# Interleaved H3 and S4D layers: one-pass gated update, angles rounded on ScalarE, and intermediate arrays stored in the order of their reading

## The chip, the cores and the metric

The kernel runs on one core of one Trainium2 chip. The core has a matrix engine (TensorE; PE in the profile, PEld for its weight loads), three engines for elementwise work (VectorE, DVE; ScalarE, ACT; GpSimd, POOL), and a SyncE queue (SP) that issues nearly all transfers; sixteen DMA engines carry them. The metric is device microseconds of one execution, lower is better. Everything is float32.

## The reference

A sequence of 2048 positions and 512 channels goes through four layers, A, B, A, B, each with a layer norm in front and a residual around it.

```python
def _A_ref(q, k, v, shift_k, ssm_k, ssm_D):      # q is layernorm(x)
    kv = short_causal_conv(k, shift_k) * v
    y = irfft(rfft(kv padded) * rfft(ssm_k padded))[:S]
    return q * (y + kv * ssm_D)
def _B_ref(u, ...):                              # u is layernorm(x)
    dt = exp(log_dt); A = -exp(log_A_real) + 1j * A_imag; C = (C_real + 1j * C_imag) * dt
    K = 2 * real(sum_n C[d, n] * exp(A[d, n] * dt * l))
    return irfft(rfft(u padded) * rfft(K padded))[:L] + u * D_skip
x = A_q
x = x + _A_ref(layernorm(x), ...); x = x + _B_ref(layernorm(x), ...)
x = x + _A_ref(layernorm(x), ...); x = x + _B_ref(layernorm(x), ...)
```

The convolution of layer A doesn't depend on x, so its result y is computed once and used twice; each use is a "gated update", x + layernorm(x) * y.

## The kernel before

Both long convolutions are Fourier transforms of length 4096 done as matrix products, in four quarters of 128 channels. A quarter's spectrum has 8 chunks; a chunk is 128 partitions (the real parts of 64 frequencies, then their imaginary parts) by 4 x 128 values, 256 KB.

The program is built of steps that a scheduler lays out ahead of the run; each engine then works its list in order.

- **Taps** (taps, 64 steps). For layer B the tap values K come from 128 modes per channel. `angles` makes phases with a matmul into PSUM (`pa`), rounds them to whole turns by adding and taking off a large constant (`MAGIC`) on DVE (tile `y`, L482), and takes the whole turns off with a second matmul by minus the identity (L483). `waves` takes Abs and two Sin on ACT; `mags` takes Exp; `products` multiplies on DVE and POOL; `contract` sums the modes on PE (`pk`), and DVE scales by 2 dt into `ks` (L528, L529), which goes to DRAM.
- **Spectra** (spectrum_quarter). Chunk by chunk ACT copies the transform `pu` into `pc` (two buffers, L244), and SP stores it into the DRAM array `spec` (L245). `spec[0]` is layer A's, from the inputs, at the start; `spec[1]` layer B's, a quarter after each 16 steps of the taps.
- **Convolutions** (convolution). 32 steps each, one chunk a step: `kab` is loaded from `spec` into both halves of the partitions, real and imaginary parts side by side, by two transfers of 256 KB, one for each half of the partitions (L259); DVE multiplies `pu` by it (`vv`, L278), ACT makes the swapped product's operand (`sw`), POOL multiplies and adds; PE transforms back. Convolution A (beside the taps) stores its result to `ya_d` in DRAM (L656); convolution B runs twice, three loads ahead, with four buffers of `kab`.
- **Gated updates** (gated_update, twice, 16 rows of 128 x 512). `yaq` is loaded from `ya_d` (L703). In one of three ways, by a table of letters, a row is shifted by minus its mean (`nm`) and multiplied by y into `ut`: on DVE in one pass (L714), or ACT and POOL (L717, L720), or POOL twice (L719, L720). DVE then adds ut times the inverse deviation (`rs`) to x, with the row's sum (L721), and ACT squares for the variance (L723). A `normalizer` per 8 rows makes nm, rs and nb.

The four transfers rows_d<-hl (L359), at the start, carry the modes' parameters to DRAM. SP issues its transfers in order; one that waits holds up those behind it. So does an engine's instruction that waits for a transfer.

Of the kernel before, what the change touches and what calls it, by code (L numbers as in the profile page):

```python
# [9 lines left out]
F32 = mybir.dt.float32  # L10
F32R = mybir.dt.float32r
# [9 lines left out]
NQ = 4  # L21
# [78 lines left out]
def kernel(ctx: ExitStack, tc: tile.TileContext, out, x_in, kv_in, ssmk_in, ssmd_in,  # L100
# [24 lines left out]
    TP = (0, 1)  # L125
    WAYS1 = "cbcdcbcdcbcdcbcd"
    WAYS2 = "bcdbcbcbbcbbcbcb"
    NORM1 = "SVSVSVSVSVSVSVSV"
# [71 lines left out]

    def normalizer(t0, n, st=None):
# [16 lines left out]
    def spectrum_quarter(which, q, src, pool, zlast, zb, tag):  # L220
        z = pool.tile([128, 64, 32, 2], F32, name="zk", tag="z", bufs=zb)
        dr = pool.tile([1, 128], F32, name="dr", tag="dr", bufs=1)
        nc.sync.dma_start(dr, (ssmd_in, dsk_in)[which][:, 128 * q:128 * q + 128])
        for g in range(4):
            kk = pool.tile([128, 512], F32, name="kk", tag="kk", bufs=3 - which)
            nc.sync.dma_start(kk, src[4 * q + g])
# [12 lines left out]
        for c in range(NCH):  # L239
            pu, ins = f2_chunk(z, c, None, tag)  # L240
            if c == NCH - 1:
                zlast.append(ins)
            pc = pool.tile([128, CK * 128], F32, name="pc", tag="pc", bufs=2)
            S.copy(pc, pu.rearrange("p k c -> p (k c)"))  # L244
            nc.sync.dma_start(spec[which][q][c], pc)  # L245
            yield
# [3 lines left out]
    def convolution(which, pools, steps, finish, lag, ahead, nk, ns, nw, inplace, add_dve, zlast=None, late_step=None, first_b=False):  # L250
# [3 lines left out]
        def load(s):  # L254
            q, c = divmod(s, NCH)
            pool = pools["conv"]
            kab = pool.tile([128, 2, CK, 128], F32, name="kab", tag="kab", bufs=nk)
            for h in range(2):
                (G if first_b and s < GL else nc.sync).dma_start(kab[64 * h:64 * h + 64].rearrange("p r k c -> p r (k c)"),  # L259
                                  spec[which][q][c].rearrange("(r k) x -> k r x", r=2))  # L260
# [73 lines left out]
    G.memset(warm, 0.0)  # L334
    S.activation(warm, warm, AF.Exp)
    dt = gp.tile([128, 4], F32, name="dt")
    nc.sync.dma_start(dt, ldt_in)
    nc.sync.dma_start(flat(cr), cr_in)
# [7 lines left out]
    dt2 = gp.tile([128, NQ, 32], F32, name="dt2")  # L346
    halfpi = gp.tile([128, 1], F32, name="halfpi")
    G.memset(halfpi, math.pi / 2)

    minus = gp.tile([128, 128], F32R, name="minus")  # L350
    G.dma_start(minus, minus_in)

# [14 lines left out]
    across = lambda t_: t_[:, :, None].to_broadcast([128, 4, 128])  # L367
    S.activation(dt, dt, AF.Exp)
    S.activation(la, la, AF.Exp)
# [33 lines left out]
    V.scalar_tensor_tensor(t1, t3, 0.5, t1, op0=ALU.mult, op1=ALU.add)  # L403
    V.tensor_add(t2, t2, t1)

# [11 lines left out]
    nc.sync.dma_start(flat(dt2), ldtb_in[:, None, :].to_broadcast([4, 32, 128]))  # L417
    S.activation(dt2, dt2, AF.Exp)
    V.tensor_scalar_mul(dt2, dt2, 2.0)
    nctx.close()  # L420
# [22 lines left out]
    rows, ms, xys, pks, angs = {}, {}, {}, {}, {}  # L443
    NXY = 2
    NM1 = 9
    NM2 = 5
# [27 lines left out]
    def angles(gi, k):  # L474
        h, s = divmod(k, 2)
        hs = slice(64 * h, 64 * h + 64)
        pa = pp.tile([128, 512], F32, name="pa", tag="pa", bufs=NPA)
        T.matmul(pa, rows[gi][hs, 0, :], tabs["tt"][hs, 8 * s:8 * s + 8, :], start=True, stop=False,
                 skip_group_check=True)

        y = wk.tile([128, 512], F32R, name="y", tag="y", bufs=2)
        V.tensor_scalar(y, pa, MAGIC, MAGIC, op0=ALU.add, op1=ALU.subtract)  # L482
        T.matmul(pa, minus, y, start=False, stop=True, skip_group_check=True)  # L483
        angs[gi, k] = pa

    def waves(gi, k):
# [4 lines left out]
        S.activation(co, rv, AF.Abs)  # L491
        for i in (S.activation(tt[:, 1, :, 1:65], rv, AF.Sin, scale=TWO_PI),  # L492
                  S.activation(co, co, AF.Sin, scale=-TWO_PI, bias=halfpi)):  # L493
            after(i, last_exp[0])
            last_sin[0] = i
# [15 lines left out]
    def contract(gi, k):  # L511
# [10 lines left out]
        if k < 3:  # L522
            return
        q, g = divmod(gi, 4)
        ks = wk.tile([128, 64, 8], F32, name="ks", tag="ks", bufs=2)
        d2 = dt2[:, q, 8 * g:8 * g + 8][:, :, None].to_broadcast([128, 8, 32])
# [62 lines left out]
    with ExitStack() as actx:  # L589
# [107 lines left out]
    def gated_update(buffer, spare, rnd, load_x=False):  # L697
        yas = []
        for k in range(4):
            if load_x:  # L700
                nc.sync.dma_start(x[:, 4 * k:4 * k + 4, :], x_in[:, 4 * k:4 * k + 4, :])
            ya = buffer(k)
            nc.sync.dma_start(ya.rearrange("p g t c -> p g (t c)"),  # L703
                              ya_d[:, :, 128 * k:128 * k + 128].rearrange("g p x -> p g x"))
            yas.append(ya)
        ways, cold = (WAYS1, WAYS2)[rnd], (WU1, WU2)[rnd]
        for t in range(16):
            pool, tag, bufs = spare[t % len(spare)]
            ut = pool.tile([128, 512], F32, name="ut", tag=tag, bufs=bufs)

            groups = lambda a: a.rearrange("p (g c) -> p g c", c=32)
            y = yas[t // 4][:, :, t % 4, :]
            if ways[t] == "c":
                V.scalar_tensor_tensor(groups(ut), groups(x[:, t, :]), nm[:, t:t + 1], y, op0=ALU.add, op1=ALU.mult)  # L714
            else:
                if ways[t] == "b":
                    S.activation(ut, x[:, t, :], AF.Identity, bias=nm[:, t:t + 1])  # L717
                else:
                    G.tensor_scalar(ut, x[:, t, :], nm[:, t:t + 1], None, op0=ALU.add)  # L719
                G.tensor_mul(groups(ut), groups(ut), y)  # L720
            V.scalar_tensor_tensor(x[:, t, :], ut, rs[:, t:t + 1], x[:, t, :], op0=ALU.mult, op1=ALU.add,  # L721
                                   accum_out=mv[:, t, 0:1])
            S.activation(ut, x[:, t, :], AF.Square, scale=-512.0, bias=mv[:, t, 0:1], accum_out=mv[:, t, 1:2])  # L723

# [15 lines left out]
    own = [(xp, "ut", 3)] * 3  # L740
    def normalized(rows):
        for t in rows:
            if t % UN == UN - 1:
                last_root[0] = normalizer(t + 1 - UN, UN)

    with ExitStack() as yctx:
        yp = sbuf(yctx, "yp", "right")
        normalized(gated_update(lambda k: yp.tile([128, 16, 4, 32], F32, name="yaq", tag="yaq", bufs=NYA),
                                own + [(yp, "ut", 16 - 4 * NYA)] * (16 - 4 * NYA), 0, True))
    bq = sbuf(ctx, "conv_q", "right")  # L750
    pools = {}
    turn = {"u": 0, "zu": 0}


# [7 lines left out]
    def steps_b(rnd, q):  # L762
# [3 lines left out]
        def norm(c):  # L766
            for t in (2 * c, 2 * c + 1):
                eng = "S" if q > 1 else NORMQ[rnd][t] if q else (NORM1, NORM2)[rnd][t]
                if eng != "S":
# [76 lines left out]
    normalized(gated_update(lambda k: rotating("u", [128, 16, 4, 32], "yaq", 3),  # L846
                            own + [(pools["conv"], "vv", NSB)] * NSB + [(pools["conv"], "sw", NSB)] * NSB, 1))
    for _ in conv_b(1):
# [66 lines left out]
```

## Time and profile before

| | |
|---|---|
| median of 3 runs | 800.36 us (798.78 to 801.9) |
| the profiled execution | 805.59 us, of which its span is 803.8 us |
| moved by DMA | 135.47 MB, mean 169 GB/s |
| mean granted TensorE clock | 0.877 |

The profile is of one execution. A row of a table by stretches has the stretch in us, its length, each engine's busy time with its count of instructions, the granted TensorE clock, the busy share of the 16 DMA engines, and GB/s. A group of instructions has its line, engine, operation, out<-in, shapes and count, then the busy time in all and the mean ns of one, then the engine's idle time just before them. A row of the SP queue has the start, the time and the transfer.

### The profile page before, as it was taken

To read this page: it belongs to the slowest core of one execution; us is meant where nothing else is said; L and a number is where in the kernel's file an instruction comes from. 1 tells how busy PE (TensorE), PEld (TensorE's weight loads), DVE (VectorE), ACT (ScalarE), POOL (GpSimd) and SP (SyncE) were. 2 spreads that over 40 slices of the span, in tenths; PEclk is the share of its full clock that TensorE was granted. 3 is DMA by queue.
4 is the path that set the end of the run, shared out by engine and by line. 5 is a ranking of instruction groups with operands and counts; after the bars stand their busy time and mean duration, and the time that the engine had idled before them with its cause. 6 is when DMAs were issued, how large, how long until landed. Compare 5 with 4: busy or idle time off the path is not lost. (4 is left out here: it accounts for less than half of the span.)

```text
span 803.8 us, 14448 instructions
## 1 busy us (share of the span) xinstructions
PE 635.2 (79%) x5064; PEld 447.3 (56%) x5064; DVE 621.3 (77%) x939; ACT 477.7 (59%) x879; POOL 533.7 (66%) x496
## 2 busy tenths in 40 slices
PE   3378696688799989999889863599789750998996
PEld 2255565356567747767556442386657620476673
DVE  7757979998967967647759499845668889878776
ACT  4035355345378875776785765649746525878573
POOL 4965778776778965838956277316665836288783
PEclk9676599868999999999899665789989995899999
DMA  9577177367477463664441593147987642068792
GB/s 326 188 247 270 40 241 254 108 200 254 146 215 203 127 182 110 182 171 123 115 131 34 174 341 105 46 129 199 233 200 183 159 103 54 1 164 223 201 252 105
DMA packets 89612, 135.47 MB, mean 169 GB/s; under 512 B 8508, under 2 KB 37700, under 8 KB 89028
## 3 DMA queue, kind: packets, MB, share of 16 engines
q1 hardware_dynamic: 88644, 132.13, 56.5%
q0 software_dynamic: 896, 2.43, 1.1%
q8 instruction: 40, 0.66, 0.4%
q14 instruction: 32, 0.26, 0.1%
HBM read 98.87 MB, written 35.65 MB: 167 GB/s over the span
## 5 line engine op out<-in xcount | busy, mean ns | idle before, releaser
L280 POOL TENSOR_TENSOR sw<-sw,kab 128x512 f32<-128x512 f32 x96 | 124.4, 1302 | 67.6 <-ACT sw L277 59.6
L196 PEld LDWEIGHTS pu<-zu,w 128*128 128x128 f32 x768 | 95.7, 193 | 52.9 <-DVE vv L278 18.6
L196 PE MATMUL pu<-zu,w 128*128 128x128 f32 x768 | 109.5, 285 | 15.1 <-DVE vv L278 12.8
L504 POOL TENSOR_TENSOR xy<-tt,m 128x512 f32<-128x512 f32 x64 | 84.9, 1327 | 53.5 <-ACT tt L493 23.8
L171 PE MATMUL pf<-kk,wz 128*128 128x256 f32 x256 | 86.3, 481 | 41.8 <-POOL kk L236 25.3
L278 DVE TENSOR_TENSOR vv<-pu,kab 128x512 f32<-128x512 f32 x96 | 64.9, 679 | 63.9 <-ACT sw L277 27.0
L290 PE MATMUL pi<-vv,mm 128*128 128x128 f32 x768 | 107.3, 285 | 3.5 <-DVE vv L278 2.6
L281 POOL TENSOR_TENSOR vv<-vv,sw 128x512 f32<-128x512 f32 x76 | 98.8, 1303 | 13.6 <-DVE vv L278 10.3
L290 PEld LDWEIGHTS pi<-vv,mm 128*128 128x128 f32 x768 | 96.5, 197 | 15.0 <-issue 9.1
L276 ACT ACTIVATE sw<-pu 64x512 f32<-64x512 f32 x96 | 57.0, 594 | 63.3 <-PE pu L196 60.8
L171 PEld LDWEIGHTS pf<-kk,wz 128*128 128x128 f32 x256 | 56.7, 237 | 62.3 <-POOL kk L236 33.3
L491 ACT ACTIVATE tt<-pa 128x512 f32<-128x512 f32 x64 | 38.3, 599 | 82.1 <-PE pa L483 72.3
L196 PE MATMUL pu<-zk,w 128*128 128x128 f32 x512 | 78.3, 307 | 6.4 <-DVE zk L191 4.2
L196 PEld LDWEIGHTS pu<-zk,w 128*128 128x128 f32 x512 | 72.7, 217 | 15.6 <-DVE zk L191 6.3
L505 DVE TENSOR_TENSOR tt<-tt,m 128x512 f32<-128x512 f32 x64 | 79.9, 1248 | 0.9 <-ACT tt L493 0.4
L244 ACT COPY pc<-pu 128x512 f32<-128x512 f32 x64 | 37.4, 591 | 57.3 <-PE pu L196 35.3
L506 DVE SCALAR_TENSOR_TENSOR xy<-tt,m 128x256 f32<-128x256 f32 x64 | 51.5, 805 | 25.7 <-ACT tt L492 15.3
L468 ACT ACTIVATE m<-pm 128x512 f32<-128x512 f32 x96 | 53.8, 604 | 22.6 <-PE pm L466 21.6
L483 PE MATMUL pa<-y,minus 128*128 128x512 f32 x64 | 37.1, 588 | 32.0 <-DVE y L482 30.5
L311 PE MATMUL po<-w,w 128*64 128x512 f32 x192 | 55.4, 655 | 7.3 <-DVE w L305 7.0
L519 PE MATMUL pk<-xy,tt 128*32 128x64 f32 x2048 | 50.5, 242 | 13.3 <-DVE ks L529 9.0
L519 PEld LDWEIGHTS pk<-xy,tt 128*32 128x32 f32 x2048 | 37.7, 122 | 39.1 <-issue 28.9
(139 smaller groups left out, 1295.4 us busy)
## 6 DMA issues: line engine op xcount, KB each, us to landing
kab<-spec SPq DMA_DIRECT2D x188, 256.0 KB, 4.0
spec<-pc SPq DMA_DIRECT2D x64, 256.0 KB, 2.7
kvt<-kv_in SPq DMA_DIRECT2D x16, 624.0 KB
yaq<-ya_d SPq DMA_DIRECT2D x8, 1024.0 KB, 10.6
kk<-ssmk_in SPq DMA_DIRECT2D x16, 256.0 KB, 2.9
kv_d<-u SPq DMA_DIRECT2D x16, 256.0 KB, 7.5
kdram<-ks SPq DMA_DIRECT2D x64, 64.0 KB, 1.8
kk<-kdram SPq DMA_DIRECT2D x16, 256.0 KB, 2.7
```

Of the source, the lines that this page charges most:

```text
L171: yield T.matmul(o, w, rhs, start=True, stop=True)
L196: ins = T.matmul(pu[:, i, :], w2[:, c * CK + i, :], z[:, :, c * CK + i, :], start=True, stop=True)
L276: S.mul(sw[0:64], pu[64:128], -1.0)
L278: V.tensor_mul(vv, pu, kabs[s][:, 0])
L280: (V if last else G).tensor_mul(sw, sw, kabs[s][:, 1])
L281: (V if last or s % add_dve == add_dve - 1 else G).tensor_add(vv, vv, sw)
L290: i1s[t] = T.matmul(pi[:, i, :], mm[:, c * CK + i, :], vvs[t][:, i, :], start=True, stop=True)
L311: ins = T.matmul(po[64 * a:64 * a + 64], w4, ws[g][:, :, 16 * a:16 * a + 16, :].rearrange("p x t r -> p t x r"), start=True, stop=True, ti ...
L468: i = S.activation(m, pm, AF.Exp)
L504: G.tensor_mul(xy[:, :, :, 32:64], tt[:, :, :, 1:33], m1[:, :, 32:64][:, None].to_broadcast([128, 2, 8, 32]))
L505: (G if (4 * gi + k) % E2P == E2P - 1 else V).tensor_mul(e2, e2, m2[:, None].to_broadcast([128, 2, 8, 32]))
L519: T.matmul(pk[32 * i4:32 * i4 + 32, 2 * k + i, :], e2[:, r, 4 * i + i4, :], xy[:, r, 4 * i + i4, :], start=r == 0, stop=r == 1, tile_posit ...
```

## The change

It has six parts.

1. **Gated update in one pass.** ACT makes `ut` = 1 + rs * y; DVE makes x = (x + nm) * ut with the row's sum. The result lacks the row's mean, which the next layer norm doesn't see; `off` keeps the sum of both means, and ACT adds it to whole rows in the last convolution (its third quarter). In the second update the last 8 rows get their statistics from DVE instead of ACT's square.
2. **Angles.** ACT adds MAGIC (activation Identity with a bias), DVE forms (y - MAGIC) - pa in one pass, and the second matmul goes; Abs and Sin read SBUF, not PSUM.
3. **2 dt inside log|C|.** log 2 + log dt is added to the logarithm of C's magnitude at the start; the copies of `pk` are plain ones, one on DVE and one on ACT.
4. **Spectrum as it is read.** `spec` keeps real and imaginary parts of a frequency side by side in DRAM: [chunk, 64, 2, 512]. The store swaps the two outer dimensions, and one transfer with a source broadcast to both halves of the partitions loads `kab`.
5. **y as it is read.** `ya_d` is [4, 128, 16, 128]: it is written in pieces of 512 B, and each of yaq's loads reads 8 KB in a row.
6. The last spectrum quarter's `pc` takes the nine buffers of a tile of the taps that is done with.

```diff
-    spec = [[dram.tile([NCH, 128, CK * 128], F32, name=f"spec{i}_{q}") for q in range(NQ)] for i in range(2)]
+    spec = [[dram.tile([NCH, 64, 2, CK * 128], F32, name=f"spec{i}_{q}") for q in range(NQ)] for i in range(2)]
-    ya_d = dram.tile([16, 128, 512], F32, name="ya_d")
+    ya_d = dram.tile([4, 128, 16, 128], F32, name="ya_d")
...
+            if which == 1 and q == NQ - 1:
+                pc = wk.tile([128, CK * 128], F32, name="pc", tag="m1", bufs=NM1)
+            else:
+                pc = pool.tile([128, CK * 128], F32, name="pc", tag="pc", bufs=2)
             S.copy(pc, pu.rearrange("p k c -> p (k c)"))
-            nc.sync.dma_start(spec[which][q][c], pc)
+            nc.sync.dma_start(spec[which][q][c].rearrange("k r x -> r k x"), pc)
...
-            for h in range(2):
-                (G if first_b and s < GL else nc.sync).dma_start(kab[64 * h:64 * h + 64].rearrange("p r k c -> p r (k c)"),
-                                  spec[which][q][c].rearrange("(r k) x -> k r x", r=2))
+            (G if first_b and s < GL else nc.sync).dma_start(
+                kab.rearrange("p r k c -> p (r k c)"),
+                spec[which][q][c].rearrange("k r x -> k (r x)")[None].to_broadcast([2, 64, 2 * CK * 128]))
...
-    V.tensor_add(t2, t2, t1)
+    V.tensor_scalar(ldt, ldt, math.log(2.0), None, op0=ALU.add)
+    for g in range(4):
+        V.scalar_tensor_tensor(t2[:, g], t2[:, g], ldt[:, g:g + 1], t1[:, g], op0=ALU.add, op1=ALU.add)
...
-        y = wk.tile([128, 512], F32R, name="y", tag="y", bufs=2)
-        V.tensor_scalar(y, pa, MAGIC, MAGIC, op0=ALU.add, op1=ALU.subtract)
-        T.matmul(pa, minus, y, start=False, stop=True, skip_group_check=True)
+        y = wk.tile([128, 512], F32, name="y", tag="y", bufs=NY)
+        S.activation(y, pa, AF.Identity, bias=magic)
+        V.scalar_tensor_tensor(y, y, MAGIC, pa, op0=ALU.subtract, op1=ALU.subtract)
...
-        V.tensor_mul(kv_[:, :, 32:64], pk[:, :, 0:32], d2)
-        V.tensor_mul(kv_[:, :, 31::-1], pk[:, :, 32:64], d2)
+        V.tensor_copy(kv_[:, :, 32:64], pk[:, :, 0:32])
+        S.copy(kv_[:, :, 31::-1], pk[:, :, 32:64])
...
-            nc.sync.dma_start(ya_d[4 * q + g], ya)
+            nc.sync.dma_start(ya_d[:, :, 4 * q + g].rearrange("k p x -> p k x"), ya.rearrange("p (k x) -> p k x", k=4))
...
+            S.activation(groups(uts[t]), yas[t // 4][:, :, t % 4, :], AF.Identity, scale=rs[:, t:t + 1], bias=1.0)
...
+            V.scalar_tensor_tensor(x[:, t, :], x[:, t, :], nm[:, t:t + 1], ut, op0=ALU.add, op1=ALU.mult,
+                                   accum_out=mv[:, t, 0:1] if t < BN[rnd] else None)
+            if t < BN[rnd]:
+                S.activation(ut, x[:, t, :], AF.Square, scale=-512.0, bias=mv[:, t, 0:1], accum_out=mv[:, t, 1:2])
             else:
+                V.bn_stats(st0[:, t, :], x[:, t, :])
...
+                    if q == 2:
+                        S.activation(x[:, t, :], x[:, t, :], AF.Identity, bias=off[:, t:t + 1])
```

What stands where on the queues follows; a row is a line, an operation, what it writes and reads, and the shape written (outermost dimension first), with the count of equal ones in a row.

First SP, near the start, which the change leaves alone: the loads of the inputs and tables (kk, w, kvt), and the first three of the stores rows_d<-hl. Before:

```order
L226 DMA kk<-ssmk_in 128x512
L359 DMA rows_d_99<-hl 8x16x1024
L667 DMA w_104<-w_in 128x1024 x2
L602 DMA kvt<-kv_in 128x1248
L223 DMA dr<-dsk_in 1x128
L226 DMA kk<-ssmk_in 128x512 x2
L359 DMA rows_d_98<-hl 8x16x1024 x2
```

The store rows_d has 8 in its outermost dimension on the DRAM side; the loads around it have 128.

Then SP from the last quarter of layer B's spectrum through the first convolution B to the first loads of the second one (spec_0 to spec_3 are the quarters; the rows of kab up to the last are the first convolution B). Before:

```order
L245 DMA spec_3_64<-pc 128x512 x8
L259 DMA kab<-spec_0_61 64x2x512 x12
L259 DMA kab<-spec_1_62 64x2x512 x6
L703 DMA yaq<-ya_d 128x16x128
L259 DMA kab<-spec_1_62 64x2x512 x2
L703 DMA yaq<-ya_d 128x16x128
L259 DMA kab<-spec_1_62 64x2x512 x8
L259 DMA kab<-spec_2_63 64x2x512 x14
L703 DMA yaq<-ya_d 128x16x128
L259 DMA kab<-spec_2_63 64x2x512 x2
L259 DMA kab<-spec_3_64 64x2x512 x16
L259 DMA kab<-spec_0_61 64x2x512 x8
```

With the change:

```order
L252 DMA spec_3_64<-pc 2x64x512 x8
L265 DMA kab<-spec_0_61 128x1x1024 x6
L265 DMA kab<-spec_1_62 128x1x1024 x3
L707 DMA yaq<-ya_d 128x2048
L265 DMA kab<-spec_1_62 128x1x1024 x2
L707 DMA yaq<-ya_d 128x2048
L265 DMA kab<-spec_1_62 128x1x1024 x3
L265 DMA kab<-spec_2_63 128x1x1024 x7
L707 DMA yaq<-ya_d 128x2048
L265 DMA kab<-spec_2_63 128x1x1024
L265 DMA kab<-spec_3_64 128x1x1024 x8
L265 DMA kab<-spec_0_61 128x1x1024 x4
```

The order is the same; each pair of loads is one transfer, and the store writes 2 x 64 x 512 where it wrote 128 x 512. The first two loads of convolution B (four transfers before) stand on POOL's queue. The source of a load, which these rows don't show, is 64 x 2 x 512 before and 2 x 64 x 1024 now, with step zero in the dimension of 2.

Last, DVE in the first gated update, among the last taps (tt, xy, y, ks) and the spectrum's transposes (zk). Before:

```order
L482 TENSOR_SCALAR y<-pa 128x512 x2
L714 SCALAR_TENSOR_TENSOR ut<-x,nm,yaq 128x512 x2
L505 TENSOR_TENSOR tt_225<-tt_225,m_4394 128x16x32
L721 SCALAR_TENSOR_TENSOR x,mv<-ut,rs,x 128x512 x2
L528 TENSOR_TENSOR ks<-pk,dt_135 128x8x32
L529 TENSOR_TENSOR ks<-pk,dt_135 128x8x32
L506 SCALAR_TENSOR_TENSOR xy<-tt_225,m_4402 128x8x32
L721 SCALAR_TENSOR_TENSOR x,mv<-ut,rs,x 128x512 x2
```

With the change:

```order
L489 SCALAR_TENSOR_TENSOR y<-y,pa 128x512
L729 SCALAR_TENSOR_TENSOR x,mv<-x,nm,ut 128x512 x3
L512 SCALAR_TENSOR_TENSOR xy<-tt_230,m_4380 128x8x32
L511 TENSOR_TENSOR tt_230<-tt_230,m_4376 128x16x32
L729 SCALAR_TENSOR_TENSOR x,mv<-x,nm,ut 128x512 x2
L512 SCALAR_TENSOR_TENSOR xy<-tt_224,m_4384 128x8x32
L729 SCALAR_TENSOR_TENSOR x,mv<-x,nm,ut 128x512 x2
```

The passes that wrote ut are gone from DVE; x takes one pass a row.

More of the change, by code (lines that the diff above doesn't have):

```diff
@@ L125 @@
     TP = (0, 1)
[L126 to L127 removed]
+    GA = 3
+    BN = (16,8)
     NORM1 = "SVSVSVSVSVSVSVSV"
@@ L199, in f2_chunk @@
         return pu, ins
+    off = cpool.tile([128, 16], F32, name="off")
     def normalizer(t0, n, st=None):
@@ L444 @@
     NXY = 2
+    NY = 2
     NM1 = 9
@@ L702, in gated_update @@
             ya = buffer(k)
[L703 to L704 removed]
+            nc.sync.dma_start(ya.rearrange("p g t c -> p (g t c)"), ya_d[k].rearrange("p g x -> p (g x)"))
             yas.append(ya)
[L706 to L723 removed]
@@ new lines, in gated_update, with factor @@
+        cold = (WU1, WU2)[rnd]
+        groups = lambda a: a.rearrange("p (g c) -> p g c", c=32)
+        uts = {}
+        def factor(t):
+            pool, tag, bufs = spare[t % len(spare)]
+            uts[t] = pool.tile([128, 512], F32, name="ut", tag=tag, bufs=bufs)
+            S.activation(groups(uts[t]), yas[t // 4][:, :, t % 4, :], AF.Identity, scale=rs[:, t:t + 1], bias=1.0)
+        if rnd == 0:
+            G.tensor_scalar(off, nm, -1.0, None, op0=ALU.mult)
+        else:
+            for t0 in range(0, 16, HN):
+                G.tensor_sub(off[:, t0:t0 + HN], off[:, t0:t0 + HN], nm[:, t0:t0 + HN])
@@ L740, with normalized @@
     own = [(xp, "ut", 3)] * 3
-    def normalized(rows):
+    def normalized(rows, rnd):
         for t in rows:
             if t % UN == UN - 1:
-                last_root[0] = normalizer(t + 1 - UN, UN)
+                last_root[0] = normalizer(t + 1 - UN, UN, None if t < BN[rnd] else lambda i: st0[:, i, :])
     with ExitStack() as yctx:
@@ L767, in norm @@
             for t in (2 * c, 2 * c + 1):
+                nb = nbs[0]
+                if rnd == 1 and q > 1:
+                    nb = nbs[1]
+                    if q == 2:
+                        S.activation(x[:, t, :], x[:, t, :], AF.Identity, bias=off[:, t:t + 1])
                 eng = "S" if q > 1 else NORMQ[rnd][t] if q else (NORM1, NORM2)[rnd][t]
@@ L846 @@
     normalized(gated_update(lambda k: rotating("u", [128, 16, 4, 32], "yaq", 3),
-                            own + [(pools["conv"], "vv", NSB)] * NSB + [(pools["conv"], "sw", NSB)] * NSB, 1))
+                            own + [(pools["conv"], "vv", NSB)] * NSB + [(pools["conv"], "sw", NSB)] * NSB, 1), 1)
+    nbs.append(cpool.tile([128, 16], F32, name="nb2"))
+    G.tensor_mul(nbs[1], off, rs)
+    G.tensor_sub(nbs[1], nb, nbs[1])
     for _ in conv_b(1):
```

31 lines of the change are left out of this document (15 added, 16 removed).

## The prediction

> **What bounds the kernel now.** I read the page's head, then the chain of work that ended last, then busy time by stretches.
>
> ```profile
> span 803.8 us, 14448 instructions
> PE 635.2 (79%) x5064; PEld 447.3 (56%) x5064; DVE 621.3 (77%) x939; ACT 477.7 (59%) x879; POOL 533.7 (66%) x496
> DVE 14%; PE 14%; issue 7%; ACT 5%; POOL 5%; DMA 3%; SPq 0%; DVEq 0%; POOLq 0%; ACTq 0%
> ```
>
> PE and DVE share the chain and the DMA has 3% of it: today this is a kernel of engines. (The chain covers the second half; records are missing before.) The next table cuts the span where the spectra's transfers begin and end: 0 to 47 setup; to 210 the spectrum of layer A is stored; to 413 convolution A loads it, and half of layer B's spectrum is stored; to 544 the tail of the taps, the first gated update and the other half; to 641 the loads of the first convolution B; to 706 its end and the second gated update; then the second convolution B. The last three columns are the granted clock, the share of the 16 DMA engines, and GB/s.
>
> ```profile
> 0.00:47.00 47.00, 18.92 (x72) 14.20 (x72) 32.24 (x44) 12.53 (x19) 30.21 (x40) 0.85 0.73 248
> 47.00:210.00 163.00, 129.47 (x1036) 89.34 (x1036) 146.34 (x186) 77.19 (x134) 120.27 (x107) 0.79 0.60 196
> 210.00:413.00 203.00, 186.36 (x1829) 135.09 (x1828) 145.47 (x205) 146.23 (x254) 145.56 (x137) 0.97 0.57 163
> 413.00:544.00 131.00, 94.32 (x853) 66.28 (x852) 99.33 (x149) 78.99 (x156) 68.09 (x63) 0.77 0.43 131
> 544.00:641.00 97.00, 83.39 (x542) 62.03 (x540) 67.94 (x116) 64.08 (x120) 66.71 (x59) 0.95 0.81 201
> 641.00:706.00 65.00, 34.82 (x156) 17.73 (x152) 58.65 (x151) 37.84 (x90) 30.40 (x31) 0.79 0.20 50
> 706.00:804.00 98.00, 87.92 (x587) 62.59 (x585) 71.30 (x93) 60.81 (x110) 72.45 (x64) 0.99 0.71 194
> ```
>
> DVE fills 47 to 210, PE the three convolutions, DVE the gated updates. But the DMA engines are never far off: 0.57 to 0.81 of them are busy while spectra move. So the first question on this change is how many DMA engines its new transfers use, and only then what it saves on DVE and PE.
>
> **What one transfer gets of the DMA engines.** Almost every transfer of the kernel before has 32, 64 or 128 entries in its outermost dimension, on both sides. One large one hasn't: the store rows_d<-hl (L359), 512 KB, goes out as 8 x 16 x 1024, outermost 8. It is issued at 12.95 and at 21.95; after that SP issues nothing until 31.4 (the second of the pair). The queue's rows and the stretches behind them:
>
> ```profile
> 12.95 0.65 SPq L359 DMA_DIRECT2D rows_d<-hl  x1
> 18.15 2.77 SPq L226 DMA_DIRECT2D kk<-ssmk_in  x2
> 21.95 10.01 SPq L359 DMA_DIRECT2D rows_d<-hl  x2
> ...
> 20.00:22.00 2.00, 0.52 (x3) 0.12 (x1) 2.00 (x2) 0.37 (x1) 2.00 (x3) 1.00 1.03 421
> 22.00:23.00 1.00, 0.00 (x0) 0.00 (x0) 1.00 (x2) 0.00 (x0) 1.00 (x1) 0.93 0.97 380
> 23.00:24.00 1.00, 0.00 (x0) 0.00 (x0) 1.00 (x2) 0.00 (x0) 1.00 (x2) 0.50 0.62 250
> 24.00:25.00 1.00, 0.00 (x0) 0.00 (x0) 1.00 (x2) 0.20 (x1) 1.00 (x1) 0.50 0.49 196
> 25.00:26.00 1.00, 0.03 (x1) 0.03 (x1) 1.00 (x2) 0.00 (x0) 1.00 (x3) 0.50 0.52 205
> 26.00:27.00 1.00, 1.00 (x3) 0.82 (x4) 1.00 (x2) 0.00 (x0) 1.00 (x1) 0.50 0.53 214
> 27.00:28.00 1.00, 1.00 (x4) 0.82 (x3) 1.00 (x2) 0.00 (x0) 1.00 (x2) 0.50 0.47 190
> 28.00:29.00 1.00, 1.00 (x4) 0.82 (x3) 1.00 (x1) 0.00 (x0) 0.83 (x1) 0.50 0.28 115
> ```
>
> Until 23 the queue drains on all engines (1.03, 0.97), at 421 / (16 x 1.03) = 25.5 KB per us and engine. From 24 to 28 exactly half are left (0.49, 0.52, 0.53, 0.47), at 190 / (16 x 0.47) = 25.3 each. The rows from 24 to 29 carry 196 + 205 + 214 + 190 + 115 = 920 KB, about the two stores' 1,049 KB. I read it so: a transfer is dealt over as many engines as its outermost dimension has entries, always the same first ones; two stores of outermost 8 put 131 KB extra on each of eight engines, 5.2 us at 25.3. That is what the half share lasts.
>
> The change makes two frequent transfers with an outermost dimension of 2: the spectrum's store (2 x 64 x 512 on the DRAM side) and the load of kab (a source broadcast to 2 x 64 x 1024). By this reading both run on the same **two** engines of sixteen.
>
> The Trainium skill, "DMA: Bandwidth & Descriptors", section "Why a DMA increments its semaphore by 16 and not by 1", states the same as a rule: the largest number up to 16 that divides the slowest dimension of both sides, on the lowest-numbered engines. The half share agrees for 8; no run shows 2. That page's table of specifications gives some 27 GiB/s (29 KB per us) for an engine; by it a load of kab would take 9.0 us and the sum below come to about 1,430; the rows give 25.3, and I go by them.
>
> **The change part by part.** First the sizes.
>
> ```profile
> q1 hardware_dynamic: 88644, 132.13, 56.5%
> kab<-spec SPq DMA_DIRECT2D x188, 256.0 KB, 4.0
> spec<-pc SPq DMA_DIRECT2D x64, 256.0 KB, 2.7
> 531.88 12.41 SPq L245 DMA_DIRECT2D spec<-pc  x8
> L259 SPq DMA_DIRECT2D kab<-spec x188: 573/580/4378, 210.0 to 779.5; - x188
> ```
>
> *Load of kab.* 512 KB per step in one transfer instead of two of 256 KB that land 4.0 us after issue. On two engines: 262.1 KB each / 25.3 = **10.4 us**, for a step that now takes (641 - 544) / 30 = 3.2 us. 96 loads: 995 us. *Store of a spectrum chunk.* 131.1 KB on each of two engines: **5.2 us**; 64 stores: 332 us. Both bounds of the rate: above, 214 / 8 = 26.7 if just eight engines carried the best half-share row (9.8 us a load); below, the last stretch of the table, mostly kab loads, 194 / (16 x 0.71) = 17.1 (15.3 us a load, 7.7 a store). I take 25.3, since two engines can't crowd each other as sixteen do there.
>
> All other SP transfers still use sixteen engines, but each puts a sixteenth on the crowded two and lands only when that is through. By stretch, with what stays in force:
>
> - 0 to 47: no spectrum moves, 47.
> - 47 to 210: the pair gets 32 stores, 166, and its part of the rest, (163 x 196 KB - 32 x 262) / 16 / 25.3 = 58: 224 at least. At most 163 + 166 = 329, if nothing lay beside the stores. In each quarter's eight stores ACT stands at the copy into the two buffers of pc, and PE behind it, while DVE's and POOL's gating of kv goes on; so nearer the lower end: **240**.
> - 210 to 413: 32 loads 332 + 16 stores 83 + rest (203 x 163 - 16,777 - 4,194) / 16 / 25.3 = 30, together 444; the engines' 203 lies beneath. DVE's product with kab waits in order, and behind it the taps' products, so a few gaps: **460**.
> - 413 to 544: pair 83 + 30, less than the engines' 131. The first gated update gives 7 back (below); the last eight stores take 42 where they took 12.4 to issue, and the last landing 2, so 28 more, and the loads of kab stand behind them on SP: 131 - 7 + 28 = **152**.
> - 544 to 641: 30 loads 311 + three yaq loads 8 = **319**.
> - 641 to 706: the second update gives 5 back; the four loads issued there (42) fit beneath: **60**.
> - 706 on: 28 loads 290 + output stores 5 = **295**, then the 20 us that now follow the last load's landing (803.8 - 779.5 - 4.0).
>
> Sum 47 + 240 + 460 + 152 + 319 + 60 + 295 + 20 = 1,593. The profiled execution was 805.59 us, 1.8 over its span, and 5.2 over the median of the runs, 800.36: **1,590**.
>
> *The rest of the change*, from the groups of instructions (the first three rows in the first gated update, the fourth in the second) and the waits:
>
> ```profile
> 467.00:512.00 45.00, 19.48 (x260) 12.94 (x259) 45.00 (x59) 23.89 (x50) 36.34 (x28) 0.65 0.56 173
> L714 DVE SCALAR_TENSOR_TENSOR ut<-x,nm,yaq 128x512 f32<-128x512 f32 x8 | 14.9, 1899 | 0.0
> L720 POOL TENSOR_TENSOR ut<-ut,yaq 128x512 f32<-128x512 f32 x8 | 11.9, 1498 | 1.0 <-ACT ut L717 1.0
> L714 DVE SCALAR_TENSOR_TENSOR ut<-x,nm,yaq 128x512 f32<-128x512 f32 x6 | 7.5, 1295 | 0.0
> L723 ACT ACTIVATE ut<-x,mv 128x512 f32<-128x512 f32 x32 | 22.9, 715 | 28.2 <-DVE x L721 28.1
> L626 DVE BATCH_NORM_STATS2 st<-xt 128x6 f32<-128x512 f32 x16 | 10.6, 665 | 0.0
> L483 PE MATMUL pa<-y,minus 128*128 128x512 f32 x64 | 37.1, 588 | 32.0 <-DVE y L482 30.5
> L491 ACT ACTIVATE tt<-pa 128x512 f32<-128x512 f32 x64 | 38.3, 599 | 82.1 <-PE pa L483 72.3
>   ACT pc L244: 20.5, 7
>   DMA kab<-spec: 42.0, 22
> ```
>
> First update: DVE, full for 45 us, loses 8 passes, 14.9; ACT gains 13 factors of about 0.7, 9, and the new rounding: 24 becomes some 38. So 45 falls to 38: 7 (bounds 0 and 15). Second: DVE loses 7.5 and POOL's contention, gains 8 statistics x 0.67 = 5.3: 5 (0 to 8). The angles: PE loses 37 us, ACT gains 64 x 0.6 = 38 and dearer reads, DVE swaps one pass for one. The stores of ya in 512 B pieces, the copies of ks, log 2 dt, nine buffers for the last pc (of ACT's 20.5 us of waits for spec stores) and ACT's 16 additions of the offset (11 us): I count all at nothing, because the engines wait for the pair anyway; without that cover they are worth what the first rival says.
>
> **Rivals.** *The transfers spread over sixteen engines after all* (faster): half a share was another queue's tail, or the pair changes from transfer to transfer. Against it, 920 KB came out at half share with nothing else issued. Then -7, -5, the angles -5 (between -20 and +10: PE is full for much of 210 to 413, ACT's added latency eats it), fewer waits for spec stores -3 and for kab -5 of 42, offset +2: 800 - 23 = 777. It decides if the dealing is by the total number of pieces (128) and not by the outermost count. *Only the store narrows* (slower): the zero-step dimension of the broadcast doesn't count and kab is dealt by 64. Then 47 + 240, 203 + 2 bursts x 19 = 241, 152, and the last 260 less 5 and 5 for kab: 930. The trace has no broadcast large enough to tell. *The pair is also slow* (17.1 KB per us): 47 + 331 + 671 + 171 + 472 + 60 + 436 + 20 = 2,208; it is the upper end of the main case.
>
> **How the numbers follow.** Two engines for both 0.85, store alone 0.06, no narrowing 0.08, anything else 0.01. The forecast is the likeliest, 1,590. Its low end: every burst hidden (224, 444, 131, 55) gives 1,535, and at 26.7 the four transfer-bound stretches lose 67: 1,470. Its high end 2,200. That holds about 0.94 of the main case, 0.80 in all. A measurement of this kernel can tell about 0.5%, 4 us: faster 0.08, within it 0.01, slower 0.91.
>
> **What would show it.** Right: kab lands more than 10 us after issue in the convolutions; in the first convolution B the DMA share is near 2/16 = 0.13 and some 50 GB/s, where 0.81 and 201 stood; the chain is mostly "DMA kab<-spec"; every engine is under half busy; setup unchanged. Wrong: a share over 0.5 in the convolutions, or kab landing in 4 us (first rival); stores late but kab prompt (second). If loads take 15 us, the rate was wrong, not the mechanism.

## The result and the profile after

| | before | after |
|---|---|---|
| median of the runs made side by side | 801.13 us (4 runs, 798.78 to 805.56) | 1604.98 us (4 runs, 1602.92 to 1607.36) |
| ratio, 95% interval | | 1.998 (1.989 to 2.006) |
| the profiled execution (its span) | 805.59 us (803.8) | 1603.58 us (1601.7) |

The forecast was 1,590. Some executions of any of these kernels come out 1 to 2% longer, among them the profiled one with both transfers wide (813.12 us); medians and ratios below leave these out, while the 808 of the expectations is a median with them. The page of the changed kernel, in the parts that were read of before: span, busy time, the DMA queue, and the chain that ended last, by engine and by line.

```profile
span 1601.7 us, 14220 instructions
PE 789.0 (49%) x5000; PEld 554.7 (35%) x5000; DVE 575.4 (36%) x920; ACT 543.4 (34%) x977; POOL 487.1 (30%) x476
q1 hardware_dynamic: 63548, 132.05, 23.4%
DMA 67%; PE 10%; ACT 6%; DVE 5%; issue 5%; SPq 4%; POOL 3%; DVEq 0%; POOLq 0%; ACTq 0%
DMA kab<-spec 38%; DMA spec<-pc 14%; DMA out_dram<-yo 3%; DMA kk<-kdram 3%; PE pf L171 3%; PE pu L196 2%; DMA yaq<-ya_d 2%; DMA xt<-x_in 2%; DMA u<-kv_d 1%; PE po L318 1%; DMA kdram<-ks 1%; SPq L660 1%; PE pm L473 1%; PE pk L525 1%; DMA kk<-ssmk_in 1%
```

The same 132 MB move, in fewer packets, and yet the chain went from 3% DMA to 67%, and no engine is busy for half the span. Here are the stretches, cut at the same events as the prediction's steps (columns as there):

```profile
0.00:53.00 53.00, 20.08 (x71) 15.14 (x72) 39.51 (x51) 14.37 (x22) 34.19 (x45) 0.81 0.69 237
53.00:280.00 227.00, 139.57 (x1022) 96.85 (x1021) 136.88 (x183) 93.45 (x161) 110.50 (x100) 0.69 0.41 133
280.00:748.00 468.00, 239.70 (x1929) 172.62 (x1929) 147.56 (x214) 180.38 (x307) 154.01 (x151) 0.69 0.21 73
748.00:888.00 140.00, 79.26 (x735) 54.43 (x733) 62.19 (x116) 94.35 (x188) 36.51 (x39) 0.72 0.34 117
888.00:1211.00 323.00, 130.83 (x544) 96.15 (x544) 72.48 (x119) 56.40 (x101) 66.81 (x60) 0.62 0.16 61
1211.00:1298.00 87.00, 35.67 (x128) 19.00 (x129) 46.38 (x148) 43.38 (x91) 13.12 (x21) 0.70 0.11 37
1298.00:1584.00 286.00, 133.97 (x538) 94.44 (x536) 62.57 (x84) 58.20 (x105) 66.87 (x60) 0.63 0.15 61
1584.00:1602.00 18.00, 9.94 (x40) 6.08 (x40) 7.89 (x9) 2.93 (x5) 5.08 (x4) 0.77 0.24 91
```

In the two convolutions B the DMA share is 0.16 and 0.15, where 0.81 and 0.71 stood, at 61 GB/s. The pace of single loads is seen at their readers: DVE's product of each step (start, time, and in brackets the idle time before it and what ended it).

```profile
1161.92 0.69 DVE L285 TENSOR_TENSOR vv<-pu,kab 128x512 f32<-128x512 f32 x1 [9.25 <-DMA kab<-spec]
...
1171.86 0.69 DVE L285 TENSOR_TENSOR vv<-pu,kab 128x512 f32<-128x512 f32 x1 [6.89 <-DMA kab<-spec]
1181.80 0.69 DVE L285 TENSOR_TENSOR vv<-pu,kab 128x512 f32<-128x512 f32 x1 [6.97 <-DMA kab<-spec]
```

A load of 524.3 KB every 9.94 us; if two engines carry it, that is 262.1 / 9.94 = 26.4 KB per us and engine (25.3 was taken). Who waits, in total, times, and at longest:

```profile
DVE vv L285 <- DMA kab<-spec: 473.7, 60, 19.3
POOL sw L287 <- DMA kab<-spec: 374.7, 53, 11.1
...
ACT pc L251 <- DMA spec<-pc: 189.8, 35, 26.9
```

DVE waited 14.0 us for kab before, and ACT 20.5 for the stores.

### The profile page after: what moved, and what is told of

Its sections match the earlier page's. It is cut to its first block, busy times and chain, and to the rows that moved or that the text cites. A ratio compares the mean times of both kernels' runs of the same rounds, so it can differ in the third digit from the quotient of the medians.

```text
span 1601.7 us, 14220 instructions
## 1 busy us (share of the span) xinstructions
PE 789.0 (49%) x5000; PEld 554.7 (35%) x5000; DVE 575.4 (36%) x920; ACT 543.4 (34%) x977; POOL 487.1 (30%) x476
## 4 chain that ended last, share of the span: by engine, by line
DMA 67%; PE 10%; ACT 6%; DVE 5%; issue 5%; SPq 4%; POOL 3%; DVEq 0%; POOLq 0%; ACTq 0%
DMA kab<-spec 38%; DMA spec<-pc 14%; DMA out_dram<-yo 3%; DMA kk<-kdram 3%; PE pf L171 3%; PE pu L196 2%; DMA yaq<-ya_d 2%; DMA xt<-x_in 2%; DMA u<-kv_d 1%; PE po L318 1%; DMA kdram<-ks 1%; SPq L660 1%; PE pm L473 1%; PE pk L525 1%; DMA kk<-ssmk_in 1%
## 5 line engine op out<-in xcount | busy, mean ns | idle before, releaser
L297 PE MATMUL pi<-vv,mm 128*128 128x128 f32 x768 | 156.4, 371 | 214.0 <-DVE vv L285 164.7
L297 PEld LDWEIGHTS pi<-vv,mm 128*128 128x128 f32 x768 | 141.0, 275 | 234.7 <-issue 110.7
L196 PE MATMUL pu<-zu,w 128*128 128x128 f32 x768 | 153.2, 360 | 112.9 <-DVE vv L285 112.7
L196 PEld LDWEIGHTS pu<-zu,w 128*128 128x128 f32 x768 | 136.2, 264 | 170.6 <-DVE vv L285 116.7
L171 PE MATMUL pf<-kk,wz 128*128 128x256 f32 x256 | 99.9, 541 | 114.9 <-POOL kk L239 89.8
L318 PE MATMUL po<-w,w 128*64 128x512 f32 x192 | 81.6, 954 | 80.2 <-DVE vv L285 62.4
L298 ACT COPY ie<-pi 128x512 f32<-128x512 f32 x64 | 37.3, 583 | 221.7 <-PE pi L297 221.5
L511 DVE TENSOR_TENSOR tt<-tt,m 128x512 f32<-128x512 f32 x64 | 66.5, 1039 | 52.6 <-ACT tt L499 51.5
L473 PE MATMUL pm<-tg,rw 64*128 64x512 f32 x96 | 50.4, 586 | 62.6 <-ACT pc L251 57.6
L171 PE MATMUL pf<-u,wz 128*128 128x256 f32 x168 | 55.4, 470 | 36.3 <-DMA u<-kv_d 23.3
```

Of the source, the lines that this page charges most:

```text
L171: yield T.matmul(o, w, rhs, start=True, stop=True)
L196: ins = T.matmul(pu[:, i, :], w2[:, c * CK + i, :], z[:, :, c * CK + i, :], start=True, stop=True)
L297: i1s[t] = T.matmul(pi[:, i, :], mm[:, c * CK + i, :], vvs[t][:, i, :], start=True, stop=True)
L318: ins = T.matmul(po[64 * a:64 * a + 64], w4, ws[g][:, :, 16 * a:16 * a + 16, :].rearrange("p x t r -> p t x r"), start=True, stop=True, ti ...
L473: mt = T.matmul(pm, rows[gi][hs, 1, :], rhs, start=True, stop=True)
L511: (G if (4 * gi + k) % E2P == E2P - 1 else V).tensor_mul(e2, e2, m2[:, None].to_broadcast([128, 2, 8, 32]))
```

## The experiments

The theory: a transfer uses as many DMA engines as its outermost dimension has entries, so store and load of the spectrum share two. The rivals were that only one of the two is narrow, that the broadcast's zero step or the new layout is slow by itself, or that another part of the change shares in the loss. All kernels compute the whole reference. In this section a time that stands with a ratio is the median of six or more executions; the others, but for the changed kernel's, are of one profiled execution, which does for effects of 5% and more. A ratio is to the kernel before, run beside that version, with its 95% interval.

**One transfer at a time.** First, the load made wide, the store left as changed:

```diff
-            (G if first_b and s < GL else nc.sync).dma_start(
-                kab.rearrange("p r k c -> p (r k c)"),
-                spec[which][q][c].rearrange("k r x -> k (r x)")[None].to_broadcast([2, 64, 2 * CK * 128]))
+            for h in range(2):
+                (G if first_b and s < GL else nc.sync).dma_start(
+                    kab[64 * h:64 * h + 64].rearrange("p r k c -> p (r k c)"),
+                    spec[which][q][c].rearrange("k r x -> k (r x)"))
```

> The changed kernel with kab loaded by two transfers whose outermost dimension is 64 on both sides; the spectrum's store stays 2 x 64 x 512. By the theory (a transfer uses as many DMA engines as its outermost dimension has entries; 2 for store and load alike) only the store is left on two engines: the price of the second rival, 930 us (870 to 990), kab landing again in some 4 to 6 us in the convolutions B, whose 32 steps take about 100 us each, while the 8 stores of a spectrum quarter still take 5 us each. Rival: something else in the new loads or stores is slow (the order of the pieces in DRAM, or the broadcast makes no difference): 1,600 stays.

Then the store made wide, the load left as changed:

```diff
-            nc.sync.dma_start(spec[which][q][c].rearrange("k r x -> r k x"), pc)
+            for r in range(2):
+                nc.sync.dma_start(spec[which][q][c][:, r], pc[64 * r:64 * r + 64])
```

> The changed kernel with the spectrum's store as two transfers of 64 x 512; the load stays one transfer with the broadcast source. Theory: the stores' 64 x 5.2 = 332 us leave the two engines, of which the four quarters at the start (227 down to about 165 us) and half of those beside convolution A (468 to some 380) were on the path, and the first convolution B starts some 20 us earlier: about 1,430 (1,370 to 1,480), the two convolutions B still at 9.8 us a load. Rival (the store is what is slow, and loads are late only behind it): below 1,000.

Then both edits together:

> The changed kernel with both as two wide transfers each; all other parts of the change stand. Theory: no transfer is narrow, so the rest of the change shows: 777 us (765 to 790), DMA share above 0.5 while spectra move. Rival (the loss is from the gated update, the angles or the layout of y): stays far above 800.

And the kernel before with these lines of the change alone (the layout of spec, its store, its load):

> The kernel before with part 4 of the change alone (the layout of the spectrum in DRAM, its 2 x 64 x 512 store and the broadcast load). Theory: the pair of DMA engines sets the time whatever the rest is: 1,600 to 1,640. Rival (another part has a share in the loss): below 1,500.

| store, load: entries | time |
|---|---|
| 2, 2 (the changed kernel) | 1604.98 |
| 2, 2 (the kernel before with part 4 alone) | 1608.22 |
| 64, 2 | 1435.86 |
| 2, 64 | 945.54 |
| 64, 64 | 804.11, ratio to before 1.0009 (0.9966 to 1.0053) |

Part 4 alone does it all. The stretch of layer A's spectrum and most of the first convolution B, first with the load wide, then with the store wide:

```profile
52.00:279.00 227.00, 143.64 (x1044) 99.27 (x1046) 137.55 (x183) 94.56 (x163) 111.17 (x100) 0.67 0.41 133
672.00:775.00 103.00, 77.31 (x500) 57.01 (x501) 67.06 (x114) 52.04 (x94) 64.48 (x57) 0.87 0.73 187
```

```profile
52.00:212.00 160.00, 122.25 (x1052) 88.24 (x1051) 137.84 (x180) 93.19 (x162) 117.61 (x103) 0.77 0.64 190
727.00:1027.00 300.00, 119.52 (x520) 87.10 (x519) 69.63 (x116) 60.94 (x113) 65.91 (x60) 0.65 0.16 61
```

Each narrow transfer lengthens its own stretch. With the narrow store the spectrum takes 227 us, as in the changed kernel; with the narrow load it takes 160. From the first load on SP to DVE's last product with kab, the first convolution B lasts 107 us with the narrow store and 317 with the narrow load, where it was 100 in the kernel before and is 323 in the changed one (the second row of each pair ends a little ahead of that product). The narrow load costs 1435.86 - 804.11 = 632 us, the narrow store 945.54 - 804.11 = 141; together they cost 801, some 28 more than the sum.

**The count of entries itself.** Here the spectrum lies in DRAM in A blocks with a gap after each, so that the dimensions can't merge; load and store, two transfers each, have A entries outermost and no zero step (A = 2, 4, 8):

```diff
-    spec = [[dram.tile([NCH, 64, 2, CK * 128], F32, name=f"spec{i}_{q}") for q in range(NQ)] for i in range(2)]
+    spec = [[dram.tile([NCH, A, 64 // A + 1, 2, CK * 128], F32, name=f"spec{i}_{q}") for q in range(NQ)] for i in range(2)]
...
+                nc.sync.dma_start(spec[which][q][c][:, :64 // A, r], pc[64 * r:64 * r + 64])
...
+                    spec[which][q][c][:, :64 // A].rearrange("a k r x -> a k (r x)"))
```

> The changed kernel with the spectrum cut in DRAM into 4 blocks with a gap after each, so that load and store, two transfers each and without the zero step, have 4 entries in their outermost dimension. Theory (as many DMA engines as entries): 512 KB a step on four engines at 26.7 KB per us, 4.9 us where the engines need 3.2: about 970 us (930 to 1,020), loads 4.9 us apart in the convolutions B. Rival (only the broadcast's zero step narrows a load, or there is no such count): about 808, or 1,600 if the gaps cost as much as the two entries.

> As with four blocks, but two: load and store have 2 entries in their outermost dimension, a plain one of two blocks with a gap, and no broadcast; each is two transfers. Theory (the count of entries alone narrows a transfer): the changed kernel's time again, 1,600 us (1,550 to 1,660), loads of 512 KB 9.8 us apart in the first convolution B. Rival (the changed load is slow because of its zero step, which reads every row twice, and four blocks were slow because of their gaps): well under 1,300.

> The same with eight blocks. Theory: 512 KB on eight engines take 2.5 us, less than the 3.2 us that a step of the convolution takes on the other engines, so most is covered: 820 us (805 to 860), and the chain of waits has little of kab's transfer. Rival (blocks with gaps cost something of their own, which the time at four blocks, 1,045 where 970 was expected, would come from): 870 or more.

Measured: 1643.14 us with two blocks, 1044.75 with four, 845.71 with eight. The zero step is not needed for the loss: with two plain blocks the loads of the first convolution B follow each other 9.9 us apart, as in the changed kernel. The readers of the loads with four blocks:

```profile
794.50 0.69 DVE L287 TENSOR_TENSOR vv<-pu,kab 128x512 f32<-128x512 f32 x1 [1.99 <-DMA kab<-spec]
799.51 0.69 DVE L287 TENSOR_TENSOR vv<-pu,kab 128x512 f32<-128x512 f32 x1 [4.32 <-DMA kab<-spec]
804.45 0.69 DVE L287 TENSOR_TENSOR vv<-pu,kab 128x512 f32<-128x512 f32 x1 [1.84 <-DMA kab<-spec]
```

5.0 us a load, half of 9.94: 131.1 / 5.0 = 26.2 KB per us for each of four engines. With eight the transfer (2.5 us, an estimate by the same pace) fits beneath the engines' step of 3.2, and DMA is 10% of the chain:

```profile
DMA 10%; PE 10%; ACT 7%; POOL 5%; issue 5%; DVE 4%; SPq 1%; DVEq 0%; POOLq 0%; ACTq 0%
```

So the pace goes with the count. The totals do less well: four blocks came out 25 us above the range that was expected, two blocks 38 above the changed kernel, eight blocks 42 above the version with both wide. Whether the gaps or the doubled number of narrow transfers cost this was not separated.

**What the rest of the change is worth.** The first rival had priced a version with wide transfers at 777 us; it ran at 804.11 (its profiled execution at 813.12; that of before was 5 us over its median too). Its stretches, and behind them those of the kernel before from the first convolution B on, cut at the same events (first loads, the next norm's statistics, the next layer's first input u, its first swapped product, the end):

```profile
0.00:53.00 53.00, 20.03 (x68) 14.88 (x69) 39.26 (x51) 13.90 (x22) 34.38 (x45) 0.81 0.68 237
53.00:218.00 165.00, 128.04 (x1049) 91.07 (x1048) 136.69 (x179) 92.71 (x161) 117.18 (x103) 0.74 0.61 183
218.00:420.00 202.00, 180.84 (x1778) 131.37 (x1777) 142.14 (x198) 165.00 (x285) 146.76 (x138) 0.97 0.63 167
420.00:543.00 123.00, 87.52 (x857) 63.63 (x855) 77.51 (x136) 102.25 (x196) 46.18 (x49) 0.79 0.46 141
543.00:661.00 118.00, 94.66 (x596) 66.57 (x592) 83.09 (x145) 67.02 (x124) 75.11 (x69) 0.91 0.67 171
661.00:687.00 26.00, 9.70 (x16) 3.47 (x16) 23.52 (x94) 16.14 (x36) 0.75 (x4) 0.74 0.30 83
687.00:708.00 21.00, 16.76 (x68) 9.24 (x68) 10.21 (x27) 20.88 (x46) 4.40 (x10) 0.76 0.01 2
708.00:811.00 103.00, 90.24 (x580) 64.75 (x580) 72.44 (x94) 63.97 (x115) 73.51 (x65) 0.95 0.66 184
```

```profile
544.00:657.00 113.00, 96.53 (x616) 68.92 (x612) 81.91 (x144) 70.09 (x130) 75.22 (x66) 0.95 0.72 178
657.00:690.00 33.00, 7.46 (x10) 2.87 (x11) 32.76 (x92) 17.09 (x43) 16.37 (x14) 0.59 0.32 78
690.00:703.00 13.00, 11.21 (x51) 5.84 (x50) 10.84 (x29) 11.83 (x32) 3.98 (x8) 1.00 0.00 0
703.00:804.00 101.00, 90.92 (x606) 64.72 (x605) 72.38 (x94) 63.73 (x115) 74.00 (x65) 0.99 0.69 188
```

The stretches of the gated updates gain what was forecast: 131 became 123 and 33 became 26. But the setup went from 47 to 53, the first convolution B from 113 to 118, and the stretch between the second update and the next product from 13 to 21. In a shorter execution (800.21 us, with the logarithm of the next experiments) the setup again takes 53 us, the first convolution B 117, the second update 26 and the stretch behind it 21; but layer A's spectrum takes 153 there, not 165 (163 before), so that one differs between executions. Between the second update and the next product ACT is busy 20.88 of 21 us, where it had been 11.83 of 13; the additions of the offset stand among the inputs u, one of the four groups being this:

```profile
687.25 1.26 ACT L795 ACTIVATE u<-x,nb,rs 128x128 f32<-128x128 f32 x3
688.46 2.56 ACT L789 ACTIVATE x<-x,off 128x512 f32<-128x512 f32 x4
690.93 3.94 ACT L795 ACTIVATE u<-x,nb,rs 128x128 f32<-128x128 f32 x10
...
708.39 0.59 ACT L285 ACTIVATE sw<-pu 64x512 f32<-64x512 f32 x1
```

In the setup two things on DVE looked guilty: four passes that add 2 dt (5.0 us where one took 1.1), and a product that waits for a store to land, with two transposes of the spectrum behind it that stood ahead of it before:

```profile
24.86 5.02 DVE L415 SCALAR_TENSOR_TENSOR t<-t,ldt,t 128x128 f32<-128x128 f32 x4
...
44.49 0.69 DVE L614 TENSOR_TENSOR u<-kvt 128x512 f32<-128x512 f32 x1 [8.71 <-DMA kv_d<-u]
45.10 1.31 DVE L191 STREAM_TRANSPOSE zk<-pf 128x512 f32<-128x512 f32 x2
```

Each was tried on the kernel with both transfers wide:

```diff
 offset on VectorE
-                        S.activation(x[:, t, :], x[:, t, :], AF.Identity, bias=off[:, t:t + 1])
+                        V.tensor_scalar(x[:, t, :], x[:, t, :], off[:, t:t + 1], None, op0=ALU.add)
 2 dt in the logarithm's scale
-    S.activation(t2, t2, AF.Ln)
+    V.tensor_scalar(ldt, dt, 2.0, None, op0=ALU.mult)
+    for g in range(4):
+        S.activation(t2[:, g], t2[:, g], AF.Ln, scale=ldt[:, g:g + 1])
...
-    for g in range(4):
-        V.scalar_tensor_tensor(t2[:, g], t2[:, g], ldt[:, g:g + 1], t1[:, g], op0=ALU.add, op1=ALU.add)
+    V.tensor_add(t2, t2, t1)
 transposes first (the third group's product is ordered behind the eighth transpose)
-                V.transpose(zr, both)
+                zts.append(V.transpose(zr, both))
...
-            e[0].tensor_mul(u, kt(3), sk(0))
+            (lambda i: after(i, zts[7]) if grp == 2 else None)(e[0].tensor_mul(u, kt(3), sk(0)))
```

> The changed kernel with both transfers wide, and the 16 additions of the offset done by VectorE instead of ScalarE. In the run with both wide ScalarE does them (11.3 us) between the second gated update and its first product of the second convolution B, which comes at 708.4 where it came at 703.2 before. Theory: these additions are the path there; VectorE stands idle then and takes about 0.42 us a row, so 6 to 8 us go: 801 us (798 to 803) beside 808. Rival (that convolution waits for its transforms on TensorE and VectorE anyway, or VectorE's rows push the transposes back as far): 808 stays.

> The changed kernel with both transfers wide, and 2 dt put inside log|C| by the scale of ScalarE's logarithm (four pieces of 128 x 128) instead of four passes of VectorE, which took 5.0 us at 25 us where one pass took 1.1 before. Theory: these passes are on the chain of the setup (the first spectrum store at 53.3 us instead of 47.1): setup back to 48 to 50, 803 us (800 to 805) beside 808. Rival (the setup is late because of the order of its loads, or the passes are covered): first store still at 53, 808 stays.

> Both transfers wide, the offset on VectorE and the logarithm's scale on ScalarE together. If both theories hold and the gains add: 808 - 7 - 5 = 796 us (791 to 800), 1% below the kernel before. If they share one wait or neither holds: 801 to 808.

> The changed kernel with both transfers wide, and one order on VectorE mended: the product of the third input group (L614), which waited 8.7 us for kv_d's store at 35 to 44 us, behind the first quarter's last two transposes (L191) instead of ahead of them, as it stands in the kernel before. Theory: this wait is why the first spectrum store comes at 53 us instead of 47: store at 47 to 49, 803 us (798 to 806), ratio to before 0.996. Rival (the store is late for another reason, or a few us at the start are lost again behind DVE, which is full up to 210): 808 stays, ratio 1.000 or more.

> The same mend, and the offset's 16 additions on VectorE too: if both gains are real and add, 798 us (794 to 802), ratio 0.992; if only the offset's, 803 (ratio near 1.000).

The second column is the first store of a spectrum; the third runs from ACT's first u of the second convolution B to its first swapped product (12.65 us before), in the profiled execution. The kernel before ran at a median of 804.30 beside the first row, 801.84 beside the next three and 801.07 beside the last two:

| both wide, and | first store | u to product | median | ratio to before (95%) |
|---|---|---|---|---|
| nothing | 53.3 | 21.1 | 804.11 | 1.0009 (0.9966 to 1.0053) |
| offset on DVE | 52.3 | 17.4 | 802.87 | 1.0025 (0.9989 to 1.0060) |
| 2 dt in the logarithm | 52.9 | 21.3 | 805.53 | 1.0051 (1.0007 to 1.0095) |
| both of these | 51.7 | 17.5 | 803.74 | 1.0006 (0.9967 to 1.0045) |
| transposes first | 50.3 | 21.3 | 809.24 | 1.0074 (1.0036 to 1.0111) |
| transposes first, offset on DVE | 51.0 | 18.0 | 805.29 | 1.0061 (1.0017 to 1.0105) |

The offset's place on the path is borne out in this stretch, at half the size that was expected. The stretch is 8.5 us longer with the offset on ACT; on DVE ACT then waits for other work (for `nb` and for TensorE), and 3.3 to 3.8 us of them come back (three pairs of rows in the table). A gain in the total is not shown: the ratios with the offset on ACT and on DVE are 1.0009 and 1.0025, 1.0051 and 1.0006, 1.0074 and 1.0061, and in each pair the intervals overlap. The rows that show the new waits, with the offset on DVE:

```profile
678.64 10.12 ACT L795 ACTIVATE u<-x,nb,rs 128x128 f32<-128x128 f32 x26 [2.99 <-DVE nb L219]
691.82 0.59 ACT L285 ACTIVATE sw<-pu 64x512 f32<-64x512 f32 x1 [3.06 <-PE pu L196]
```

The logarithm's theory fell: the passes went, and the first store stayed at 52.9. The order of the transposes gives 3 of the 6 us at that place, and the total none of it; the edit also moved the scheduler's order of the taps behind it, so its total is no clean test. What else makes the setup late, and why the first convolution B takes up to 5 us more (114 to 119 us in all these versions, 113 before), stays open. No version here is faster than the kernel before: in the profiled executions the 15 us that the gated updates gain are spent in the other stretches.

## Why the prediction was right

| step | forecast | measured |
|---|---|---|
| setup | 47 | 53 |
| spectrum of layer A | 240 | 227 |
| convolution A | 460 | 468 |
| end of the taps, first update, last stores | 152 | 140 |
| loads of the first convolution B | 319 | 323 |
| its end, the second update | 60 | 87 |
| second convolution B | 295 | 286 |
| after the last load | 20 | 18 |
| sum | 1,593 | 1,602 |

**Two engines for store and load alike** was right, and is shown: each alone made its own stretch slow, and with four entries in place of two a load took half as long. Of the signs that were named, the DMA share (0.16), the rate (61 GB/s) and the engines under half busy came. The loads of kab are 38% of the chain, not most of it (all transfers together are 67%), and the setup did change. The rule of the Trainium skill on which engines a transfer gets ("DMA: Bandwidth & Descriptors", section "Why a DMA increments its semaphore by 16 and not by 1") agrees with the paces at two and four entries (9.94 and 5.0 us a load). The same page of the Trainium skill, section "Rules for kernel authors", names this very shape, a leading zero-step broadcast of c copies, as an example. The run without a zero step shows that two plain blocks do the same.

**The rate**: 26.4 KB per us and engine against the 25.3 that the half-share stretch gave, 4% up; a load takes 9.9 us, not 10.4. By the Trainium skill's some 27 GiB/s (29 KB per us; "DMA: Bandwidth & Descriptors", section "Specifications") the estimate was 9.0 us.

**The second rival** priced a kernel with only the store narrow at 930; with the load made wide it measured 945.54. Its price was good, but its premise fell: the broadcast load is narrow.

**The term that was mis-sized**: the second update, 87 for 60. The prediction said that other transfers land only when the crowded pair is through, and counted "the four loads issued there" as beneath the update. But the fourth load of yaq, which the update needs, stands behind those four on SP's queue and on the pair. The chain, and who waits for the tile:

```profile
1232.66 6.83 ACT ut L718 x11
1239.49 0.91 ACT ut L735 x3
1240.39 26.38 DMA yaq<-ya_d
1266.79 0.73 ACT ut L718
```

```profile
  DMA yaq<-ya_d: 24.4, 2
```

26.4 us, about the whole difference. The setup was 6 us more, where the changes to it were counted at nothing: the order of the transposes gave 3 of them, part 3's passes none, and the rest is open. The stretch with the first update, 152, was 12 too high: more of the stores than was allowed lay beside the engines' work.

In the four stretches that the pair sets, the faster pace hides another error. If the pair carries everything at 26.4, its own work comes to some 215, 426, 306 and 283 us (an estimate: 224, 444, 319 and 295 of the prediction, times 25.3 / 26.4); measured were 227, 468, 323 and 286. So about 12, 42, 17 and 3 us more were spent there, where 16, 16, 0 and 0 were allowed for gaps. Whether the pair stood idle in them or some transfers were slower than 26.4 was not separated. These errors cancel, to 9 us in 1,600: that the sum came so close is luck, that it came near 1,600 is not.

**The first rival's price** failed by 27 us: its mechanism didn't come, and had it come, the time would have been 804, not 777. The updates' 12 were there (15 measured). The offset, priced at 2, stands in front of the second convolution B, whose start is 8.5 us later for it; the setup's 6 were not in the price. Of the 8 for shorter waits, some came: ACT waited 15.5 us for stores of a spectrum instead of 20.5, and DVE's product 9.6 for kab instead of 14.0. But POOL's product (`sw`) waited 27.2 for kab instead of 6.1, and a load landed 4.2 us after issue where it took 4.0, though the packets fell from 88,644 to 68,288. What these waits are worth in the total was not separated.

```profile
q1 hardware_dynamic: 68288, 132.06, 57.3%
kab<-spec SPq DMA_DIRECT2D x188, 256.0 KB, 4.2
```

The angles' 5 don't show: convolution A, where PE was fullest, takes 202 us for 203. No run separated that part.

## What to carry to other kernels

Before joining two transfers into one by a broadcast or a transposed view, look at the outermost dimension on both sides: with few entries the transfer has few engines, and here a step that lasted 3.2 us took 9.9. In a profile this is a DMA share stuck a little above k/16 for k engines (here 0.16 for two, at 61 GB/s, of which the pair's loads are 2 x 26.4 KB per us), while the chain is full of transfers; other loads, here yaq's, then wait behind them too. And work that is moved into the next stage is hidden only if it stands behind the first instruction which that stage waits for on the same engine.

## What was not expected of the hardware

While PE waited for loads, the granted clock in the three convolutions was 0.69, 0.62 and 0.63 instead of 0.97, 0.95 and 0.99, and the same 768 products took a third longer each (371 ns for 283); the first row is of the changed kernel, the second of the one with both transfers wide. In the convolutions B no cost of it shows, since the loads set the pace there; it makes PE look busier than its work (789 us for 628).

```profile
L297 PE MATMUL pi<-vv,mm 128*128 128x128 f32 x768 | 156.4, 371 | 214.0 <-DVE vv L285 164.7
```

```profile
L299 PE MATMUL pi<-vv,mm 128*128 128x128 f32 x768 | 106.7, 283 | 13.8 <-DVE vv L287 10.4
```
